# Moving loads, evictions and attention in a fused chunk-attention and swish kernel: v by whole batches, beta by rows, a 512-wide first layer at the start, attention between second layers

## The chip, the cores and the metric

The kernel runs on one core of a Trainium2 chip (trn2). The metric is the device time of one execution in microseconds (us). Executions of the kernel before vary more than most: in these studies its runs that were not marked slow lay between 333.3 and 340.1 us, and a run's time goes with the clock that TensorE was granted in it (mean 0.94 to 0.97). So every experiment below was timed against runs of the kernel before on the same chip, in the same rounds. A run is marked slow when it is more than 1.5% above the fastest of the same kernel. The clock is given as a share of full speed.

Engines are named as the profile names them: PE is TensorE (matmuls; PEld is its loading of weights), DVE is VectorE, ACT is ScalarE, POOL is GpSimd, SP is the engine that issues plain DMAs.

## The reference, cut to what matters

```python
# q, k, v: (batch 8, heads 8, seq 576, head_dim 64), float32
# attention inside chunks of 64 positions, 9 chunks per sequence
scores = (1/8) * q_c @ k_c.T            # per chunk and head, 64 x 64
attn   = softmax(scores)
x      = (attn @ v_c)                   # -> (4608 tokens, 512)
h      = x @ w_in                       # 512 -> 2048      "first layer"
g      = h * sigmoid(beta * h)          # beta: one number per hidden unit
out    = g @ w_out                      # 2048 -> 512      "second layer"
```

## The kernel before

Tokens are handled in 36 pairs of chunks (128 tokens each). Pairs are grouped in blocks: blocks 0 to 2 have 1, 1 and 2 pairs and share one tile of results, blocks 3 and 4 have 2 pairs each, and blocks 5 to 11 have 4 pairs (512 tokens). One row of a block's first layer (`emit_m`) is four matmuls for 128 hidden units. It is followed by a tanh on ACT (h * sigmoid(beta * h) is half of h * (1 + tanh(beta * h / 2)), so the kernel halves beta first) and one add-and-multiply on DVE, which I call the eviction. An attention step (`attn_step`) emits a pair's value product, and before it the scores and exponentials that it needs. `warm(n)` is n matmuls on zeros, whose results nobody uses. A pair's second layer (`emit_t`) is 16 matmuls of 512 columns.

```python
def load_vf(n, engines):                # v of one unit (2, 3 or 4 chunks), by head
    for a in range(2):
        for e in range(HS):
            for h in range(2):
                engines[i % len(engines)].dma_start(out=t[64*a:64*a+64, e, h], in_=v[...])

def emit_pv(i):                         # value product of pair i, then normalise on DVE
    ...
    if i >= EARLY:                      # EARLY = 8
        nc.sync.dma_start_transpose(out=xt_t[j][...], in_=x16...)   # DMA transpose
    else:
        x_t[i] = x16                    # later: 4 PE transposes and an ACT copy (emit_xt)

def sc_after(g):                        # after the scores of a group of three chunks
    if c == 0: load_qk(batch b+2)
    if c == 3: load_v(b+2)              # 4 DMAs on POOL, into one of three v buffers
    if c == 3: emit_T(batch b+1, first half)    # DVE transposes of q and k, 2.3 us a half
    if c == 6: emit_T(batch b+1, second half)
# main part, cut
nc.scalar.dma_start(out=beta_sb, in_=moe_beta.rearrange("(k p) -> p k", p=128))
...
ms(0, 8, 10); emit_xt(3); ms(2, 0, 8)   # ms(j, a, b): rows a to b of block j's first layer
ms(0, 10, 16); ms(1, 8, 16); ms(2, 8, 16)
...
# blocks 4 and later: attention steps are spread over first-layer rows and second layers
```

In these traces each engine takes its instructions in the order in which the program gives them (in the kernel before, ACT's first exponential, at 14.26 us, stands behind the halving of beta, at 14.13). POOL runs ahead of the others: a load that it issues waits only for its buffer to come free, and everything behind that load on POOL waits with it.

The softmax here doesn't subtract the row's maximum and nothing guards it: scores larger than these inputs give would overflow.

## Time and profile before

| | before |
|---|---|
| median of three runs | 335.48 us (335.41 to 336.15) |
| the profiled run | 338.64 us, 336.9 us of it in the span |
| PE busy | 300.8 us |
| DMA traffic | 33.2 MB, 36.7 MB read from HBM |

The profiled execution was 3 us longer than the median, though not enough to be marked slow.

From the profile page of the kernel before: the engines' busy time, and 40 slices of the span with the PE's busy share and the granted PE clock in tenths.

```profile
PE 300.8 (89%) x3130; PEld 153.3 (45%) x3130; DVE 168.8 (50%) x310; ACT 154.1 (46%) x286; POOL 52.1 (15%) x74
...
PE   6465899996738999999999998999999999999995
...
PEclk9579599997995999999999999999999999999999
```

PE is full from the middle on. The low digits are in the first five slices (to 42 us) and in the tenth to twelfth (76 to 101 us). Low PE digits are followed by a low clock.

Busy time by stretch, kernel before: stretch and its length, then busy us and counts of PE, PEld, DVE, ACT and POOL, then PE clock, DMA share and GB/s. (The share adds up the times of all packets over 16 DMA engines, so it can exceed 1.)

```profile
40.00:44.00 4.00, 4.00 (x25) 3.03 (x24) 2.00 (x5) 2.51 (x6) 0.67 (x1) 0.63 1.25 194
80.00:90.00 10.00, 7.31 (x177) 5.96 (x175) 8.60 (x16) 7.34 (x17) 4.02 (x5) 0.97 0.89 121
90.00:100.00 10.00, 4.57 (x108) 3.45 (x108) 8.44 (x19) 4.11 (x10) 0.79 (x2) 1.00 1.52 169
100.00:110.00 10.00, 7.75 (x99) 3.36 (x100) 2.87 (x5) 3.62 (x6) 0.27 (x1) 0.66 0.27 43
170.00:337.00 167.00, 159.85 (x1364) 73.69 (x1362) 75.44 (x120) 74.94 (x120) 3.41 (x4) 1.00 0.27 55
```

After 170 us PE limits. Between 80 and 100 us DVE is busy 17 of 20 us and PE only 12: DVE limits there. From 100 to 110 us no engine but PE is busy for as much as half of the time, and PE runs at clock 0.66.

The chain of waits of the kernel before, at that place: start, length, what.

```profile
92.46 0.69 DVE x_1685 L240
...
96.12 0.69 DVE x_1779 L240
...
96.83 5.37 DMA xt<-x_1779
...
102.25 1.89 PE hps L279 x4
```

The last attention result of block 5 leaves DVE at 96.8 us, its DMA transpose lands 5.4 us later, and only then can PE start block 5. Its first four matmuls take 1.89 us, twice the usual 0.86: during the idle time, at 101.0 us, the granted clock fell to 0.5.

The ACT timeline at the start of the kernel before (start, length, engine and line, what), and below it the first DVE transpose of k.

```profile
3.47 0.61 ACTq L354 DMA_DIRECT2D beta_sb<-in_moe_beta_dram  x1
...
14.13 0.22 ACT L370 ACTIVATE beta_sb<-beta_sb 128x16 f32<-128x16 f32 x1 [8.74 <-DMA beta_sb<-in_moe_beta_dram]
14.26 0.36 ACT L221 ACTIVATE et_235<-sc_201 128x256 f16<-128x256 f32 x1
```

```profile
6.92 0.63 DVE L190 STREAM_TRANSPOSE kT<-ku 128x256 f32<-128x256 f32 x1 [5.30 <-DMA ku<-in_k_dram]
```

The first q and k are there by 9 us, but the first exponential stands behind the halving of beta in ACT's order, and beta lands at 14.1 us.

### The profile page before, as it was taken

The numbers are of one execution on the slowest core, as the hardware profiler recorded it, in microseconds if no ns is written. First come the engines' busy times: TensorE is split into PE (matmuls) and PEld (weight loads), VectorE is DVE, ScalarE is ACT, GpSimd is POOL, SyncE is SP. The second block draws the span as 40 slices with busy tenths as digits, with TensorE's granted clock in tenths as the row PEclk, the third lists the DMA queues.
The fourth block names the chain that finished last, engine by engine and source line by source line (L and its number), as shares of the span: only waits on it lengthen the run. The fifth ranks groups of instructions, "written<-read, shape, count | busy, mean of one in ns | idle before, by whom it ended". The sixth has DMA issues, their size and how long they took to land.

```text
span 336.9 us, 7475 instructions
## 1 busy us (share of the span) xinstructions
PE 300.8 (89%) x3130; PEld 153.3 (45%) x3130; DVE 168.8 (50%) x310; ACT 154.1 (46%) x286; POOL 52.1 (15%) x74
## 2 busy tenths in 40 slices
PE   6465899996738999999999998999999999999995
PEld 2244585464523444444444443444444544444442
DVE  1255384567962419813871685178418604711700
ACT  1044493384543237615841672277237524823711
POOL 8352143720500500230002100000000000000000
PEclk9579599997995999999999999999999999999999
DMA  7999999999991991198012903210231113002011
GB/s 72 173 185 197 196 163 177 200 219 173 94 176 33 118 223 46 20 175 191 16 33 96 117 18 64 80 47 6 59 104 25 28 69 92 4 31 95 0 62 62
DMA packets 78450, 33.16 MB, mean 98 GB/s; under 512 B 64081, under 2 KB 70737, under 8 KB 78417
## 3 DMA queue, kind: packets, MB, share of 16 engines
q0 software_dynamic: 46080, 17.21, 46.7%
q1 hardware_dynamic: 29696, 15.34, 19.8%
q10 hardware_dynamic: 2640, 0.14, 0.6%
q8 instruction: 24, 0.39, 0.5%
q14 instruction: 10, 0.07, 0.1%
HBM read 36.71 MB, written 9.44 MB: 137 GB/s over the span
## 4 chain that ended last, share of the span: by engine, by line
PE 71%; DVE 13%; DMA 8%; ACT 2%; issue 2%; SPq 1%; ACTq 1%; DVEq 0%
PE ops L302 36%; PE hps L279 30%; DVE kT L190 4%; DVE qT L190 4%; DMA vf<-in_v_dram 3%; DMA beta_sb<-in_moe_beta_dram 3%; DVE gt L288 3%; PE x L231 2%; DMA xt<-x_1779 2%; ACT sg L287 2%; SPq L135 1%; ACTq L135 1%; PE xp L259 1%; PE wp L268 0%; DVE rd L238 0%
## 5 line engine op out<-in xcount | busy, mean ns | idle before, releaser
L279 PE MATMUL hps<-xt,w_in_104 128*128 128x512 f16 (+2 forms) x768 | 139.9, 339 | 12.5 <-DVE gt L288 5.8
L288 DVE SCALAR_TENSOR_TENSOR gt<-sg,hps 128x512 f16<-128x512 f32 (+2 forms) x192 | 103.2, 552 | 77.4 <-ACT sg L287 76.2
L287 ACT ACTIVATE sg<-hps,beta_sb 128x512 f32<-128x512 f32 (+2 forms) x192 | 108.0, 581 | 44.4 <-PE hps L279 38.7
L302 PE MATMUL ops<-w_out_105,gt 128*128 128x512 f16 x576 | 127.6, 379 | 0.0
L279 PEld LDWEIGHTS <-w_in_104 128*128 128x128 f16 x768 | 72.4, 102 | 70.4 <-issue 12.3
L302 PEld LDWEIGHTS <-gt 128*128 128x128 f16 x576 | 55.1, 98 | 64.6
L312 ACT ACTIVATE osb<-ops 128x512 f32<-128x512 f32 x36 | 21.5, 597 | 104.7 <-PE ops L302 92.8
L238 DVE RECIPROCAL rd<-x 128x8 f32<-128x8 f32 x36 | 7.0, 193 | 63.7 <-PE x L231 63.7
L190 DVE STREAM_TRANSPOSE kT<-ku 128x576 f32<-128x576 f32 (+3 forms) x18 | 20.0, 1118 | 5.3 <-DMA ku<-in_k_dram 5.3
L212 PEld LDWEIGHTS <-kT 32*64 32x64 f16 x1152 | 12.2, 109 | 19.4 <-issue 12.8
L190 DVE STREAM_TRANSPOSE qT<-qu 128x576 f32<-128x576 f32 (+3 forms) x18 | 19.7, 1104 | 1.4 <-DMA qu<-in_q_dram 1.4
L158 POOL DMA_DIRECT2D vr_107<-in_v_dram x8 | 6.8, 868 | 51.0 <-PE x L231 51.0
L268 PE MATMUL wp<-zero 128*128 128x512 f16 x26 | 11.0, 575 | 1.2 <-DVE zero L356 1.2
L158 POOL DMA_DIRECT2D vr_106<-in_v_dram x8 | 6.9, 870 | 29.9 <-PE x L231 26.7
L158 POOL DMA_DIRECT2D vr_108<-in_v_dram x8 | 6.8, 875 | 19.0 <-PE x L231 18.9
L120 POOL DMA_DIRECT2D qu<-in_q_dram x10 | 6.7, 675 | 13.7 <-DMA w_in_104<-in_moe_w_in_dram 5.9
L263 ACT COPY xt<-xp 128x512 f16<-128x512 f16 x8 | 4.7, 585 | 8.9 <-PE xp L259 8.9
L120 POOL DMA_DIRECT2D ku<-in_k_dram x10 | 7.0, 703 | 7.3 <-DMA w_out_105<-in_moe_w_out_dram 5.8
L268 PEld LDWEIGHTS <-zero 128*128 128x128 f16 x26 | 2.7, 125 | 5.0 <-issue 3.3
L114 POOL DMA_DIRECT2D ku<-in_k_dram x6 | 4.5, 745 | 1.6 <-DVE gt L288 1.1
L114 POOL DMA_DIRECT2D qu<-in_q_dram x6 | 4.5, 744 | 1.3 <-DVE gt L288 1.3
L370 ACT ACTIVATE beta_sb<-beta_sb 128x16 f32<-128x16 f32 x1 | 0.2, 217 | 8.7 <-DMA beta_sb<-in_moe_beta_dram 8.7
(259 smaller groups left out, 145.2 us busy)
## 6 DMA issues: line engine op xcount, KB each, us to landing
out_dram<-osb SPq DMA_DIRECT2D x36, 256.0 KB, 2.1
ku<-in_k_dram POOLq DMA_DIRECT2D x6, 576.0 KB, 10.3
qu<-in_q_dram POOLq DMA_DIRECT2D x6, 576.0 KB, 13.6
w_in_104<-in_moe_w_in_dram POOLq DMA_DIRECT2D x4, 512.0 KB, 11.6
w_out_105<-in_moe_w_out_dram POOLq DMA_DIRECT2D x4, 512.0 KB, 18.5
vr_108<-in_v_dram POOLq DMA_DIRECT2D x8, 144.0 KB, 7.1
vr_106<-in_v_dram POOLq DMA_DIRECT2D x8, 144.0 KB, 10.0
vr_107<-in_v_dram POOLq DMA_DIRECT2D x8, 144.0 KB, 5.8
```

Of the source, the lines that this page charges most:

```text
L114: nc.gpsimd.dma_start(out=t.rearrange("p e r d -> p e (r d)"), in_=src[b].rearrange("(e h) (p r) d -> (h p) e (r d)", h=HQ, p=32),)
L120: nc.gpsimd.dma_start(out=t[:, e], in_=src[b, e * HQ:(e + 1) * HQ, s:s + w, :].rearrange("h (p r) d -> h p (r d)", p=32),)
L158: nc.gpsimd.dma_start(out=vring[b % NVR][64 * a:64 * a + 64, e, :, :, 0:D].rearrange("p h c d -> p (h c) d"), in_=v[b, h0:h0 + 2].rearrang ...
L190: nc.vector.transpose(out=dst[n][:, sl].bitcast(FP32).rearrange("p h i r o -> p h r (i o)"), in_=a[:, sl].bitcast(FP32),)
L212: nc.tensor.matmul(out=sc[hq % 2][o0:o0 + 64, c, e, :], lhsT=kt[32 * hq:32 * hq + 32, e, cs, par], rhs=qt[32 * hq:32 * hq + 32, e, cs, par ...
L238: nc.vector.reciprocal(out=rd, in_=x[:, :, :, D:D + 1])
L268: nc.tensor.matmul(out=ps, lhsT=zero[:, 0:128], rhs=zero, start=True, stop=True)
L279: nc.tensor.matmul(out=hps, lhsT=w_in16[:, 2 * (kk % 2) + kk // 2, m * 128:(m + 1) * 128], rhs=xt_t[j][:, kk, :], start=(kk == 0), stop=(k ...
L287: nc.scalar.activation(out=sg, in_=hps, func=ACTF.Tanh, scale=beta2_sb[:, m:m + 1])
L288: nc.vector.scalar_tensor_tensor(out=gt_t[gi][:, m, col:col + n], in0=sg, scalar=1.0, in1=hps, op0=ALU.add, op1=ALU.mult,)
L302: nc.tensor.matmul(out=ops, lhsT=gt_t[gi][:, kk, col + o * 128:col + (o + 1) * 128], rhs=w_out16[:, kk, :], start=(kk == 0), stop=(kk == K ...
L312: nc.scalar.activation(out=osb, in_=ops, func=ACTF.Copy, scale=0.5)
```

## The change

Its intent is to fill the DMA engines from the first microsecond, to take beta's wait away, to save ACT and DVE instructions at the start, and to put attention where ACT and DVE are idle, which is beside second layers. The diff, cut to its core:

```diff
-    EARLY = 8
+    EARLY = 12                                   # pairs 8 to 11 too by PE transposes
-    beta_sb = const.tile([128, KFF], FP32)
+    beta_in = const.tile([32, 128], FP32)        # 16 rows of 512 B, then four 32x32
+    beta_sb = const.tile([128, 32], FP32)        # transposes and a multiply on DVE
     def load_vf(b, engines):                     # whole batch: 4 transfers of 288 KB
         for a in range(2):
             for e in range(HS):
-                for h in range(2): ... one head of one unit ...
+                engines[e % len(engines)].dma_start(out=t[64*a:64*a+64, e]..., in_=v[b, h0:h0+2]...)
...
-        ms(1, 0, 8)
         emit_T(2)
-        cast_v(2, "dve")
+        cast_v(2, nc.vector)
+        load_vf(1, [nc.sync])
+        ms(1, 0, 8)
...
-        ms(0, 8, 10)
+        warm(2)
         emit_xt(3)
         ms(2, 0, 8)
-        ms(0, 10, 16)
-        ms(1, 8, 16)
-        ms(2, 8, 16)
+        ms("all", 8, 16)                         # blocks 0 to 2 as one 512-wide product
...
-        emit_T(5, (0,))                          # (in the middle of block 3)
...
+        emit_T(5, (0,))
+        ms(4, 0, 8)
+        emit_T(5, (1,))
+        ms(4, 8, 16)                             # before: 4 attention steps inside block 4
+        for i in range(4):
+            attn_step()                          # pairs 8 to 11
+            emit_t(4 + i, 0, 9)
+            emit_xt(8 + i)
+            emit_t(4 + i, 9, 16)
         for j in range(5, NB):                   # before: attention steps spread evenly
             for m in range(KFF):
                 if m == 4:
+                    for t in pend:
+                        if npv[0] < goal: attn_step()
+                        emit_t(t)
+                elif j == 5 and m in (1, 5, 9, 12):
+                    attn_step()                  # pairs 12 to 15
+                emit_m(j, m)
```

More of the change, by code (lines that the diff above doesn't have):

```diff
@@ L44 @@
     qk_p = ctx.enter_context(tc.tile_pool(name="qk", bufs=3))
-    vf_p = ctx.enter_context(tc.tile_pool(name="vf", bufs=2))
+    vf_p = ctx.enter_context(tc.tile_pool(name="vf", bufs=1))
     qt_p = ctx.enter_context(tc.tile_pool(name="qt", bufs=2))
@@ L126, in load_qk, with load_vf @@
             dst[n] = t
-    def load_vf(n, engines):
-        b, c, cnt = units[n]
-        t = vf_p.tile([128, HS, 2, cnt, D], FP32, tag="vf", name="vf")
-        i = 0
+    def load_vf(b, engines):
+        t = vf_p.tile([128, HS, 2, BC, D], FP32, tag="vf", name="vf")
         for a in range(2):
             for e in range(HS):
-                for h in range(2):
-                    engines[i % len(engines)].dma_start(
-                        out=t[64 * a:64 * a + 64, e, h],
-                        in_=v[b, 4 * e + 2 * a + h, c * CH:(c + cnt) * CH, :].rearrange(
-                            "(c p) d -> p c d", p=CH
-                        ),
-                    )
-                    i += 1
-        v_t[n] = t
+                h0 = 4 * e + 2 * a
+                engines[e % len(engines)].dma_start(
+                    out=t[64 * a:64 * a + 64, e].rearrange("p h c d -> p (h c) d"),
+                    in_=v[b, h0:h0 + 2].rearrange("h (c p) d -> p (h c) d", p=CH),
+                )
+        v_t[b] = t
     def cast_v(n, eng):
         b, c, cnt = units[n]
-        t = v_t.pop(n)
-        for e in range(HS):
-            op = nc.gpsimd.tensor_copy if eng == "pool" else nc.vector.tensor_copy
-            op(
-                out=vring[b % NVR][:, e, :, c:c + cnt, 0:D],
-                in_=t[:, e],
-            )
+        eng.tensor_copy(
+            out=vring[b % NVR][:, :, :, c:c + cnt, 0:D].rearrange("p e h c d -> p (e h) c d"),
+            in_=v_t[b][:, :, :, c:c + cnt].rearrange("p e h c d -> p (e h) c d"),
+        )
     def load_v(b):
@@ L243, in emit_pv @@
         j, o = pair_block[i]
-        if o == 0:
+        if i == 0:
+            xs = xt_p.tile([128, KDM, 512], FP16, tag="xt", name="xt")
+            for jj in range(3):
+                xt_t[jj] = xs[:, :, blocks[jj][3]:blocks[jj][3] + blocks[jj][1] * 128]
+            xt_t["all"] = xs
+        elif i > 3 and o == 0:
             xt_t[j] = xt_p.tile([128, KDM, blocks[j][1] * 128], FP16, tag="xt", name="xt")
@@ L272, in emit_m @@
     def emit_m(j, m):
-        n = blocks[j][1] * 128
-        gi, col = blocks[j][2:]
+        n, gi, col = (512, 0, 0) if j == "all" else (blocks[j][1] * 128, *blocks[j][2:])
         if gi not in gt_t:
@@ L350, in ms, with beta_half @@
             emit_m(j, m)
+    def beta_half():
+        for g in range(4):
+            nc.vector.transpose(
+                out=beta_sb[32 * g:32 * g + 32, :], in_=beta_in[:, 32 * g:32 * g + 32]
+            )
+        nc.vector.tensor_scalar_mul(out=beta2_sb, in0=beta_sb[:, 0:KFF], scalar1=0.5)
     with tc.manual_schedule():
         load_vf(0, [nc.sync, nc.scalar])
-        nc.scalar.dma_start(out=beta_sb, in_=moe_beta.rearrange("(k p) -> p k", p=128))
-        load_vf(1, [nc.sync])
+        nc.vector.memset(beta_in, 0.0)
         nc.vector.memset(zero, 0.0)
+        nc.sync.dma_start(out=beta_in[0:KFF, :], in_=moe_beta.rearrange("(k p) -> k p", p=128))
         for i in range(NVR):
@@ L369 @@
         load_qk(3)
-        nc.scalar.activation(out=beta2_sb, in_=beta_sb, func=ACTF.Copy, scale=0.5)
+        load_qk(4)
         emit_T(0)
-        cast_v(0, "dve")
-        load_vf(2, [nc.sync])
+        cast_v(0, nc.vector)
+        beta_half()
         warm(14)
@@ L381 @@
         emit_T(1)
-        cast_v(1, "dve")
-        load_vf(3, [nc.sync])
+        cast_v(1, nc.vector)
         sc_next()
@@ L388 @@
         emit_xt(1)
+        emit_T(2)
+        cast_v(2, nc.vector)
+        load_vf(1, [nc.sync])
         ms(1, 0, 8)
-        emit_T(2)
-        cast_v(2, "dve")
         sc_next()
-        load_qk(4)
-        load_vf(4, [nc.sync])
-        cast_v(3, "pool")
+        cast_v(3, nc.gpsimd)
+        cast_v(4, nc.gpsimd)
+        load_qk(5)
+        load_v(2)
         warm(2)
@@ L400 @@
         pv_next()
-        ms(0, 8, 10)
+        warm(2)
         emit_xt(3)
         ms(2, 0, 8)
-        ms(0, 10, 16)
-        ms(1, 8, 16)
-        ms(2, 8, 16)
+        ms("all", 8, 16)
         emit_T(3)
-        load_qk(5)
-        cast_v(4, "pool")
-        load_v(2)
         for g in range(4):
@@ L436 @@
         ms(3, 14, 16)
-        emit_T(5, (1,))
+        emit_T(5, (0,))
         load_qk(6)
         load_v(3)
-        ms(4, 0, 2)
-        attn_step()
-        ms(4, 2, 6)
-        attn_step()
-        ms(4, 6, 9)
-        attn_step()
-        ms(4, 9, 11)
-        attn_step()
-        ms(4, 11, 16)
-        pend = list(range(4, 8))
+        ms(4, 0, 8)
[6 more added lines that the diff above has]
+            emit_t(4 + i, 9, 16)
+        pend = []
         for j in range(5, NB):
             goal = blocks[j + 1][0] + blocks[j + 1][1] if j + 1 < NB else NP
-            slots = []
             for m in range(KFF):
                 if m == 4:
-                    slots += [("t", t) for t in pend]
-                slots.append(("m", m))
-            need = goal - npv[0]
-            first = 1
-            span = max(1, len(slots) - 6 - first)
-            marks = {}
-            for a in range(need):
-                w = first + (a * span) // max(1, need)
-                marks[w] = marks.get(w, 0) + 1
-            for i, sl in enumerate(slots):
-                for _ in range(marks.get(i, 0)):
+                    for t in pend:
+                        if npv[0] < goal:
+                            attn_step()
+                        emit_t(t)
+                elif j == 5 and m in (1, 5, 9, 12):
                     attn_step()
-                if sl[0] == "t":
-                    emit_t(sl[1])
-                else:
-                    emit_m(j, sl[1])
+                emit_m(j, m)
             pend = list(range(blocks[j][0], blocks[j][0] + blocks[j][1]))
```

## The prediction

> **What bounds the kernel now.** From 110 us to the end TensorE is the limit: busy-by-stretch view, 160 of 167 us busy after 170 us, clock 1.00. A 512-wide matmul takes 0.216 us, so a block of four token pairs costs 13.8 us per layer; blocks take 30.5 to 32 us with attention. Most of the loss is before: TensorE is idle about 17 us of the first 50, with clock 0.5 to 0.85, and about 11 us between 70 and 105. There VectorE is the limit (8.6 of 10 us busy at 80-90). The chain of waits ends this stage in a DMA transpose (96.8 to 102.25) that leaves TensorE idle about 4.5 us and at clock 0.5 until 107.
>
> **What changes, by stage.**
>
> 1. Start. In the ACT timeline the first exponential waits for the half-beta, which waits 10.6 us for a 2048-element beta load (3.5 to 14.1). Sixteen rows of 512 B remove this. The Trainium skill (DMA: Bandwidth & Descriptors, Specifications) says transfers under 512 B fall short of line rate; 10.6 us for 8 KB agrees. But all of v (1.18 MB) now shares the DMA engines with the first q and k, so I expect the first value product at about 12.5 us, not 14.7. Then the DMA is full (about 190 GB/s to 60 us), and q of the third unit gates: it landed near 28, I expect 25-26. The transposes moved ahead of eight evictions spare part of TensorE's 2.7 us wait at 31.8. Net about 2.5 us by the third value product.
> 2. 512-wide first layer: 24 ACT and VectorE pairs (0.29 and 0.47 us on ACT, 97% busy from 44 to 52) become 8 of 0.69, and TensorE limits: 8 us become 6.9. Gain 1.3 us.
> 3. Blocks 3 and 4. Four attention steps and two whole-batch transposes (2.3 us per half) leave the first layers, where VectorE limits, for the second layers, where ACT and VectorE idle. Pairs 8 to 11 use TensorE transposes (0.4 us) instead of the late DMA transpose. From the start of block 3 (68.35) to the end of block 5's first layer I count about 69 us before and 56 after. Gain about 13.
> 4. New loss: in block 5 the attention of pair 15 stands before row 12 of 16, behind a 2.3 us VectorE transpose, and its DMA transpose (2.4 us quiet, 5 to 6 beside loads) must land in the 3.5 us of rows 12-15. TensorE should idle 3 to 6 us, with the clock falling to 0.5: loss about 6.
> 5. Steady blocks: attention before each second layer removes the VectorE/ACT stalls; blocks near 30.3 us. Gain about 4.
>
> Sum: about 15 us, nearly all on the critical path, as TensorE runs in order with little slack afterwards. Prediction 320.8 us, range 315 to 327. Faster by over 2%: 0.94; within 2%: 0.05; slower: 0.01.
>
> **What would show it.** Right: no ACT wait for beta; first value product before 13.5 us; block 3's first layer starting near 64.5; no wait for a DMA transpose before block 5; one of several us before block 6, with a clock drop; no TensorE wait on a VectorE x product in later blocks. Wrong: first score product after 12 us (v crowding q and k), third-unit transposes waiting past 29, or TensorE waiting for evictions in blocks 3 and 4 as long as before.
>
> **What would make it wrong.** v up front delaying q, k and w_in so that the start gains nothing (plus 3 us); no stall at block 6 (minus 6); evictions blocked behind the early transposes while q is in flight; v of the second batch (one buffer, copied on GpSimd) holding up the loads queued behind it.

## The result, and the profile after

| | before | after |
|---|---|---|
| median of three runs | 335.48 us (335.41 to 336.15) | 325.84 us (324.85 to 326.75) |
| ratio, 95% interval | | 0.9706 (0.9657 to 0.9755) |
| the profiled run | 338.64 us | 325.84 us |
| PE busy, mean clock | 300.8 us, 0.949 | 295.6 us, 0.963 |

A ratio is the mean time of one kernel's fast runs over that of the other's of the same rounds, so it is not quite the ratio of the medians. The kernel is 9.6 us faster. The prediction's range holds the time, but its gain of 14.7 us was half as large again as the real one.

The page of the changed kernel, as above:

```profile
PE 295.6 (91%) x3084; PEld 147.9 (46%) x3084; DVE 170.7 (53%) x297; ACT 153.8 (47%) x273; POOL 51.8 (16%) x72
...
PE   7268799987799975999999999999999999999995
...
PEclk9676999999999995999999999999999999999999
```

The deep hole of the twelfth slice is gone. There is a new one in the fifteenth and sixteenth slices, again followed by a low clock. The busy time by stretch shows both, with the columns as before:

```profile
40.00:44.00 4.00, 4.00 (x23) 1.96 (x21) 2.94 (x7) 3.08 (x7) 1.20 (x2) 1.00 1.38 183
76.00:84.00 8.00, 4.45 (x41) 3.80 (x40) 7.78 (x16) 4.28 (x11) 0.00 (x0) 1.00 1.87 180
84.00:104.00 20.00, 20.00 (x351) 10.65 (x348) 9.87 (x17) 9.17 (x19) 4.81 (x6) 1.00 1.00 145
120.00:124.00 4.00, 0.15 (x1) 0.00 (x0) 3.33 (x7) 0.69 (x2) 0.00 (x0) 0.82 1.27 157
124.00:130.00 6.00, 5.17 (x14) 1.95 (x15) 1.37 (x2) 1.51 (x3) 0.00 (x0) 0.55 0.02 4
```

In 76 to 84 us DVE is still the limit: DVE transposes of q and k (2.3 us for each half of a batch) stand among the evictions of block 4. From 84 to 104 us attention runs beside second layers and PE is never idle. From 120.2 us on PE stands still for 4.7 us; the clock falls to 0.5 at 122.6 us and stays there until 129.4 us. The chain of waits of the changed kernel says why:

```profile
118.00 1.17 DVE kT L183
119.17 1.08 DVE qT L183
...
120.31 0.69 DVE x_2120 L233
...
121.02 3.67 DMA xt<-x_2120
...
124.83 5.85 PE hps L276 x16
```

This is the stall that the prediction named. Pair 15's attention result waits for two DVE transposes, and block 6 waits for its DMA transpose. The result is there at 121.0 us, 0.85 us after block 5's last matmul, and the DMA transpose then takes 3.7 us.

At the start, the ACT and the DVE timeline of the changed kernel:

```profile
14.78 0.38 ACT L214 ACTIVATE et_224<-sc_190 128x256 f16<-128x256 f32 x1 [11.21 <-PE sc_191 L205]
```

```profile
12.65 0.63 DVE L183 STREAM_TRANSPOSE kT<-ku 128x256 f32<-128x256 f32 x1 [10.91 <-DMA ku<-in_k_dram]
```

Beta holds nothing any more, but k now lands at 12.6 us in place of 6.9, and the first exponential is half a microsecond later than before.

I cut both traces at the first matmul of each stage. The last column gives other profiles whose code in that stage is that of the kernel before, because the profile of the kernel before was a long one.

| stage, us | before | after | other profiles with the code of before |
|---|---|---|---|
| start to block 2 | 38.7 | 36.8 | 37.8, 37.4 (e1, e3) |
| block 2 to first second layer | 13.3 | 10.4 | 11.3, 11.3, 11.3 (e1, e4, e8) |
| to block 3 | 16.3 | 16.3 | |
| block 3 to the end of block 5's first layer | 68.1 | 56.6 | 68.0, 67.3 (e3, e8) |
| idle before block 6 | none | 4.7 | |
| block 6 to the end | 200.6 | 199.2 | 200.6, 200.6 (e3, e8) |

### The profile page after: what moved, and what is told of

Same layout as the page of the kernel before. It is cut to its first block, busy times and chain, and to the rows that moved or that the text cites. A ratio compares the mean times of both kernels' runs of the same rounds, so it can differ in the third digit from the quotient of the medians.

```text
span 324.1 us, 7273 instructions
## 1 busy us (share of the span) xinstructions
PE 295.6 (91%) x3084; PEld 147.9 (46%) x3084; DVE 170.7 (53%) x297; ACT 153.8 (47%) x273; POOL 51.8 (16%) x72
## 4 chain that ended last, share of the span: by engine, by line
PE 80%; DVE 9%; DMA 4%; ACT 3%; issue 1%; POOL 1%; ACTq 0%; DVEq 0%; POOLq 0%
PE ops L299 37%; PE hps L276 36%; DMA qu<-in_q_dram 3%; DVE gt L285 3%; PE x L224 2%; DVE kT L183 2%; DVE qT L183 2%; ACT sg L284 1%; DMA xt<-x_2120 1%; PE xp L257 1%; PE wp L266 1%; ACT xt L261 1%; POOL ku L121 0%; DVE rd L231 0%; DVE x_3155 L233 0%
## 5 line engine op out<-in xcount | busy, mean ns | idle before, releaser
L276 PE MATMUL hps<-xt,w_in_105 128*128 128x512 f16 (+2 forms) x704 | 133.3, 351 | 10.3 <-DMA xt<-x_2120 4.7
L299 PE MATMUL ops<-w_out_106,gt 128*128 128x512 f16 x576 | 130.3, 380 | 0.0
L284 ACT ACTIVATE sg<-hps,beta_sb 128x512 f32<-128x512 f32 (+2 forms) x176 | 105.3, 611 | 36.5 <-PE hps L276 29.0
L276 PEld LDWEIGHTS <-w_in_105 128*128 128x128 f16 x704 | 68.6, 102 | 70.7 <-issue 14.5
L299 PEld LDWEIGHTS <-gt 128*128 128x128 f16 x576 | 54.0, 98 | 61.5
L183 DVE STREAM_TRANSPOSE qT<-qu 128x576 f32<-128x576 f32 (+3 forms) x18 | 19.7, 1106 | 0.1
L205 PEld LDWEIGHTS <-kT 32*64 32x64 f16 x1152 | 11.6, 108 | 18.1 <-issue 9.5
L261 ACT COPY xt<-xp 128x512 f16<-128x512 f16 x12 | 7.0, 586 | 17.0 <-PE xp L257 17.0
L266 PE MATMUL wp<-zero 128*128 128x512 f16 x28 | 11.3, 552 | 1.3 <-DVE zero L359 1.3
L121 POOL DMA_DIRECT2D qu<-in_q_dram x10 | 6.7, 669 | 11.5 <-DVE gt L285 2.9
L121 POOL DMA_DIRECT2D ku<-in_k_dram x10 | 7.2, 726 | 5.3 <-DMA w_out_106<-in_moe_w_out_dram 2.3
## 6 DMA issues: line engine op xcount, KB each, us to landing
vr_107<-in_v_dram POOLq DMA_DIRECT2D x8, 144.0 KB, 10.2
```

The lines of the kernel that those rows point to most:

```text
L121: nc.gpsimd.dma_start(out=t[:, e], in_=src[b, e * HQ:(e + 1) * HQ, s:s + w, :].rearrange("h (p r) d -> h p (r d)", p=32),)
L183: nc.vector.transpose(out=dst[n][:, sl].bitcast(FP32).rearrange("p h i r o -> p h r (i o)"), in_=a[:, sl].bitcast(FP32),)
L205: nc.tensor.matmul(out=sc[hq % 2][o0:o0 + 64, c, e, :], lhsT=kt[32 * hq:32 * hq + 32, e, cs, par], rhs=qt[32 * hq:32 * hq + 32, e, cs, par ...
L261: nc.scalar.copy(out=xt_t[j][:, :, o * 128:(o + 1) * 128], in_=xp)
L266: nc.tensor.matmul(out=ps, lhsT=zero[:, 0:128], rhs=zero, start=True, stop=True)
L276: nc.tensor.matmul(out=hps, lhsT=w_in16[:, 2 * (kk % 2) + kk // 2, m * 128:(m + 1) * 128], rhs=xt_t[j][:, kk, :], start=(kk == 0), stop=(k ...
```

## The experiments

The prediction was a sum of five terms. The first four runs do one part of the change alone, or undo one. The next four test the reasons for what those showed. The last four put together what helped. All gave correct results. Times are medians of all runs; ratios are of fast runs alone, against the kernel before in the same rounds (one run of e3 and one of e8 were marked slow). e1 to e4 ran on one chip, e5 to e8 on a second, e9 to e11 on a third and e12 on a fourth, and the change itself was timed apart from all of them. So a difference of medians between these groups is only as good as the ratios, or the stages of the profiles, that go with it.

| run | time, us | ratio (95% interval) |
|---|---|---|
| e1 attention moves only | 327.12 | 0.9708 (0.9650 to 0.9765) |
| e2 after, rows 1, 4, 6, 8 | 323.15 | 0.9584 (0.9533 to 0.9635) |
| e3 512-wide only | 335.89 | 0.9948 (0.9888 to 1.0008) |
| e4 start only | 340.43 | 1.0087 (1.0021 to 1.0152) |
| e5 = e2 and loads held | 319.89 | 0.9540 (0.9499 to 0.9581) |
| e6 = e2 and transposes moved | 327.80 | 0.9785 (0.9727 to 0.9843) |
| e7 after, rest of v held | 333.89 | 0.9956 (0.9908 to 1.0005) |
| e8 beta by rows only | 334.27 | 0.9961 (0.9897 to 1.0025) |
| e9 = e5 and e6 | 318.73 | 0.9487 (0.9453 to 0.9521) |
| e10 = e9, v paced | 320.38 | 0.9521 (0.9486 to 0.9556) |
| e11 = e10, third batch's transposes moved | 318.90 | 0.9483 (0.9445 to 0.9521) |
| e12 = e9 with e11's last edit | 316.39 | 0.9449 (0.9401 to 0.9496) |

### e1: the attention moves alone

```diff
 (kernel before)
-    EARLY = 8
+    EARLY = 12
-    ... tail from block 3 on, as before ...
+    ... tail from block 3 on, as in the change ...
```

> The kernel before with one part alone: attention moved between second layers, whole-batch transposes moved, TensorE transposes for pairs 8 to 11. Theory (most of the gain is this part, and it also brings the new stall before block 6): about 7 to 9 us faster than before (11.5 us less between the start of block 3 and the end of block 5's first layer, 1.4 us less afterwards, 4.9 us of idle TensorE added). Rival (the gain comes from the start, and the attention move only shifts waits): within 3 us of before.

The ratio is 0.9708, the same as that of the whole change. Block 3 to the end of block 5's first layer takes 56.6 us, and PE waits 4.6 us for a DMA transpose before block 6 (total us, times, longest):

```profile
PE hps L279 <- DMA xt<-x: 4.6, 1, 4.6
```

So this part carries the gain and the new stall, and all the rest of the change adds nothing that these timings can see. (The old start is still in this kernel: its first exponential came at 11.6 us, not 14.3 as in the profile of before. The beta load's landing varies from run to run.)

### e2: pair 15 earlier

```diff
-                elif j == 5 and m in (1, 5, 9, 12):
+                elif j == 5 and m in (1, 4, 6, 8):     # (and the m == 4 branch only if pend)
```

> The changed kernel with the four attention steps of block 5 at rows 1, 4, 6 and 8 in place of 1, 5, 9 and 12. Theory (pair 15's DMA transpose is issued too late): the 4.7 us TensorE wait before block 6 goes to under 1 us, the clock stays 1.00 there, and the kernel is 5 to 7 us faster than the changed one. Rival (the transpose is held by the batch loads, whatever its place): the wait stays over 3 us.

By the medians it is faster than the change by 2.7 us, half of what I expected (by the ratios 1.3%, about 4 us; from block 2 to the end the two profiles differ by 2.6 us). The two waits on PE, of the changed kernel and of e2, from the view of who waited for whom (total us, times, longest):

```profile
PE hps L276 <- DMA xt<-x_2120: 4.7, 1, 4.7
```

```profile
PE hps L276 <- DMA xt<-x: 2.4, 1, 2.4
```

The clock stayed at 1.00 this time, and block 6 took 30.2 us in place of 32.5. But 2.4 us of waiting are left, though pair 15's attention now stands eight rows before the end of the block, and block 5's own first layer grew from 17.5 to 19.4 us. Pair 15's result was now there at 118.7 us, 4.3 us before block 5's last matmul, which would have hidden a transpose of 2.4 us. Neither theory covers this alone. The issue and landing records of the trace show the four DMA transposes of block 5's attention taking 2.5, 7.6, 10.3 and 6.5 us. Something slows them, and the same transposes took 2.4 us where nothing else moved.

### e3: the 512-wide first layer alone

```diff
 (kernel before)
-        ms(0, 8, 10); ... ms(0, 10, 16); ms(1, 8, 16); ms(2, 8, 16)
+        warm(2); ... ms("all", 8, 16)
```

> The kernel before with one part alone: rows 8 to 15 of the first layer of blocks 0 to 2 as one 512-wide product. Theory of the prediction (24 pairs of evictions become 8): 1 to 1.5 us faster than before, seen between the first 256-wide product and the first second-layer product. Rival (the 2.9 us seen there came mostly from the clock, which happened to be 1.00 instead of 0.5 after 36 us): the stretch still takes over 12 us at clock 0.5, and the time is within 1 us of before.

The stretch took 10.4 us against 11.3 us in e1, e4 and e8, which have the narrow products: 0.9 us gained. The 13.3 us of the kernel before were this profile's bad luck. Its clock was 0.63 between 40 and 44 us (the stretch above), 1.00 in the changed kernel. So both theories hold in part. The saving is real but smaller than 1.3 us, and the other 2 us between the two profiles are clock. The ratio's interval includes 1.

### e4: the start alone

```diff
 (kernel after)
-    EARLY = 12, ms("all", 8, 16), new tail
+    EARLY = 8, narrow products and the tail as before
```

> The kernel before with one part alone: v of a whole batch in four transfers up front, beta by rows, earlier transposes and load issues at the start; evictions and attention order as before. Theory: the first k transpose again starts near 12.6 us instead of 6.9, the first exponential no earlier than 14.3, block 2 starts 1 to 2 us earlier; 1 to 2 us faster than before in all. Rival (the beta wait was worth its 2 us and more): 3 us faster or more.

This kernel is slower than the one before, by 0.9%, which neither theory had. Block 2 starts at 37.0 us, 1 us earlier than the mean of 38.0 in the three profiles with the old start. The loss lies elsewhere: block 3 to the end of block 5 took 73.8 us in place of 68. With EARLY = 8, pairs 8 to 11 go by DMA transposes again, and PE waited for the last of them:

```profile
PE hps L276 <- DMA xt<-x: 11.1, 1, 11.1
```

The four transposes took 7.6, 11.8, 15.3 and 12.0 us, with batch loads in flight. In the whole change, the PE transposes of pairs 8 to 11 keep this cost away. Why the loads lay worse on these transposes than in e3 (11.6, 10.1 and 6.9 us for the last three) was not tested. The traces show one difference: when the first of the four was issued (82.1 us in e4, 81.6 in e3), a batch of q and k was still under way in e4. Its queue moved 359 packets of 2304 B from 82 to 86 us, against 73 in e3. That this is the reason is not shown.

### e5: the batch loads held back

```diff
 (e2)
+        if i == 15:          # in emit_pv, after pair 15's result
+            nc.gpsimd.tensor_copy(out=hold_sb, in_=x16[:, 0, 0, 0:1])
+            load_v(5)        # no longer issued when the scores of pair 14 are emitted
```

> The kernel with rows 1, 4, 6 and 8, and GpSimd made to read one column of pair 15's attention result before it issues the next batch of v, so that these 1.18 MB are not in flight beside the DMA transposes of pairs 13 to 15. Theory (the transposes are slow because of the batch loads in flight): the remaining 2.4 us wait before block 6 goes to under 0.5 us and the DMA transposes of pairs 14 and 15 land in 2.4 to 3 us in place of 6 and more; 2 us faster than with the rows alone. Rival (pair 15's attention result itself is late, VectorE being the limit): the wait stays over 1.5 us.

POOL issues the v of batch 5 as soon as its buffer is free, which is after pair 13's value product: in the middle of block 5's attention. The small copy makes POOL wait until pair 15's result exists, with all that stands behind it: v is issued at 117.3 us in place of 108.5, and the q and k loads that follow at 120.6 in place of 111.9. The transposes then took 2.5, 4.7, 2.4 and 2.4 us, and the wait is gone. (The one of 4.7 us had no packet of POOL's queue beside it; what slowed it stays open.) Two stretches of e5, with columns as before:

```profile
120.00:124.00 4.00, 4.00 (x20) 1.81 (x19) 3.30 (x5) 3.15 (x5) 2.10 (x3) 1.00 2.04 145
124.00:130.00 6.00, 6.00 (x103) 2.87 (x102) 3.19 (x8) 2.37 (x5) 0.76 (x1) 1.00 1.30 191
```

PE is busy throughout, at clock 1.00. The kernel is 3.3 us faster than e2 by the medians, on another chip. From block 2 to the end the profiles differ by 2.6 us, which is the wait of 2.4 us; the rest lies in the start, whose code is the same. The rival falls: pair 15's result came as late in the block as in e2 (15.2 us after block 5's start in both) and did not hold block 6. The loads in flight did. Which of them, v or the q and k behind it, was not separated.

### e6: the transposes out of block 5

```diff
 (e2)
-        if b >= 1 and c == 3: emit_T(...)      # and c == 6
+        if b >= 1 and c == 3 and b != 3: ...   # and c == 6
 ...
+        # block 6, after row 3: emit_T(first half), value product of pair 16,
+        # emit_T(second half), then second layers; the next scores one step later
```

> The kernel with rows 1, 4, 6 and 8, and the two VectorE transposes of 2.3 us each that stood in block 5 moved behind the first layer rows of block 6, beside second layers. Theory (VectorE is over its limit in block 5: 16 evictions of 0.69, 4 attention results of 0.9 and 4.7 us of transposes are 19.4 us against TensorE's 16.4): block 5's first layer takes 16.5 to 17.2 us in place of 19.4, pair 15's result comes about 2 us earlier, and the wait before block 6 falls below 1 us; 3 to 4 us faster than with the rows alone. Rival (loads in flight hold the DMA transposes whatever VectorE does): block 5 is shorter but the wait grows by as much, and the time stays within 1 us.

DVE did what I expected. Block 5's first layer took 16.9 us in place of 19.4, and pair 15's result came 3.8 us earlier, counted from block 5's start. But the DMA transposes got worse still (2.5, 7.0, 16.5 and 14.4 us):

```profile
PE hps L276 <- DMA xt<-x: 9.1, 1, 9.1
```

The kernel is slower than e2 by 4.65 us by the medians, and the intervals of the ratios lie apart; the profiled run was the slowest of six (330.61 us), so its stages may overstate the loss. The rival was right in kind, and the loss was more than it said. With DVE quicker, the transposes of pairs 14 and 15 were issued 3.9 and 6.5 us after v's first load, in place of 6.1 and 10.3 in e2, so more of the loads still lay ahead of them: a faster engine, and a slower kernel. Not all of it is explained by that: they landed 21 us after v's first load, in e2 17.

### e7: the rest of v held

```diff
 (after)
-        load_vf(0, [nc.sync, nc.scalar])
+        load_vf(0, [nc.sync, nc.scalar], 0, 2)          # chunks 0 and 1, by head
 ...
         emit_T(0)
+        nc.vector.memset(v_t[0][:, :, :, 2:BC, 0:1], 0.0)   # the DMAs wait for this write
+        load_vf(0, [nc.sync], 2, BC)
```

> The changed kernel, with v of the first unit alone (two chunks of nine) up front and the rest of v held until the first q and k have landed. Theory (v up front crowds the first q and k): the first k transpose starts near 7 us in place of 12.6, the first exponential near 10.5, the first attention result near 12 in place of 16.4, and the third comes 0.5 to 1.5 us earlier; 0.5 to 1.5 us faster than the changed kernel. Rival (the same bytes have to come by then, so all is paid back): the third attention result is within 0.3 us of 33.3 to 34.2.

The first half of the theory holds: k was transposed at 7.1 us, the first exponential came at 10.1 and the first attention result at 11.7. Then everything was lost, and 8 us more than the change. From the DVE timeline of e7:

```profile
16.96 0.82 DVE L186 STREAM_TRANSPOSE qT<-qu 128x384 f32<-128x384 f32 x1
32.05 0.56 DVE L145 CAST vr<-vf 128x768 f16<-128x768 f32 x1 [14.26 <-DMA vf<-in_v_dram]
```

The held 0.92 MB (seven ninths of 1.18 MB) were issued from 9.5 us and landed at 32 us. The packet records of the trace show how. These are counts worked out from them, for two queues: the one of POOL (q, k and the weights) and the one of SP (v).

```
us         POOL's queue: packets, median size, GB/s    SP's queue: packets, median size, GB/s
24 to 26   367  1024 B  150                            367  256 B  45
26 to 28   316  1024 B  158                            310  256 B  38
28 to 30   335  1024 B  163                            276  256 B  34
```

In this stretch the queues get nearly the same number of packets, whatever the size of a packet. The Trainium skill (DMA: Bandwidth & Descriptors, Queues, rings and completion order) says that each engine goes round its queues packet by packet, and these counts agree. (A packet of the page holds several descriptors, typically 9 to 17; whether a record of the trace is such a packet or a single descriptor, no run here shows.) So v, in packets of 256 B, gets a fifth of the bytes as long as weight packets of 1024 B are waiting. The change's transfers up front are through before the weights come. That is what they buy, and the late q and k are the price.

For a DMA transpose beside the loads, the turn by packets is only part of the account. A transpose of one pair has about 540 packets, nearly all of 256 B, on SP's queue. From 117 to 121 us of e6 the two queues moved 312 packets each, POOL's nearly all of 2304 B (q and k). But from 113 to 116 us, with two transposes or more issued and not landed, POOL's queue moved 2307 packets, most of 128 B (v), and SP's only 100. And in the changed kernel, the transpose issued at 116.2 us had its first packet 3.8 us later, beside q and k, where in e5 the last two began after 1.2 us. Turns of one packet each don't explain these stretches. That the loads slow the transposes is shown by e5; by what mechanism they hold back the first packets stays open.

### e8: beta by rows alone

```diff
 (kernel before)
-        nc.scalar.dma_start(out=beta_sb, in_=moe_beta.rearrange("(k p) -> p k", p=128))
+        nc.scalar.dma_start(out=beta_in[0:KFF, :], in_=moe_beta.rearrange("(k p) -> k p", p=128))
 ...
-        nc.scalar.activation(out=beta2_sb, in_=beta_sb, func=ACTF.Copy, scale=0.5)
+        beta_half()                       # four 32x32 transposes and a multiply on DVE
```

> The kernel before with one part alone: beta as 16 rows of 512 B and block transposes on VectorE, in the same place of the ACT queue. Theory of the prediction (4-byte elements made the load slow): it lands 3 to 5 us after its issue in place of 8 to 10.6, the first exponential starts near 10.3, limited by the first q. Rival (the load is slow because it shares the DMA engines with v, q and k and its size hardly counts): it lands 8 us or more after its issue, and the first exponential starts after 11.5 as before.

The DMA view, one line each for e8 (rows, behind four small v transfers), e1 (elements, in the same place of the queue) and the changed kernel (rows, behind large v transfers); the last number is us from issue to landing:

```profile
beta_in<-in_moe_beta_dram ACTq DMA_DIRECT2D x1, 8.0 KB, 5.1
```

```profile
beta_sb<-in_moe_beta_dram ACTq DMA_DIRECT2D x1, 8.0 KB, 8.0
```

```profile
beta_in<-in_moe_beta_dram SPq DMA_DIRECT2D x1, 8.0 KB, 10.4
```

With elements it took 8.0, 9.3 and 10.6 us in three profiles, with rows 5.1 us, so the theory of the prediction holds in size. But rows took 10.4 us as well where two v transfers of 288 KB stood ahead of them on SP's queue, so what is in flight ahead of the load or beside it counts as much (the two were not separated). In e8 the first exponential came at 10.2 us, the first attention result at 11.5, and block 2 started at 36.6 us, as early as in the changed kernel (36.8). So in this one profile the rows alone give what the change's start gives. v up front and the moved transposes add nothing to it that these profiles can see: in the six profiles with the change's start (the change, e2, e5, e6, e9 and e12) block 2 started between 35.7 and 37.7 us, 36.4 in the mean. By time the rows alone are not clear of noise: the ratio's interval includes 1.

### e9 to e12: what helped, together

> The changed kernel with rows 1, 4, 6 and 8, the held batch loads, and the two VectorE transposes moved out of block 5: both of the last two edits together. Theory (moving the transposes failed alone only because the DMA transposes then lay beside the loads; without the loads VectorE's share of block 5 counts): block 5's first layer takes about 17 us in place of 19.4, no wait before block 6, about 2 us faster than with the loads held alone, near 318. Rival (the transposes cost as much in block 6): the same as with the loads held alone.

> The kernel of the run before this one, with v of the first batch in 24 transfers by head and by unit (2, 3 and 4 chunks), paced by their issue at about 0.65 us each, in place of four large ones. Theory (four large transfers at once crowd q and k; paced ones don't, and early enough ones are done before the large weight packets take their turns): first k transpose near 7 us, first attention result near 12, third 1 us earlier than with the large transfers, 0.5 to 1.5 us faster. Rival (the later units of v get one small packet for each large weight packet, as when they were held): VectorE waits for v in the second or third copy, no gain or a loss.

> The kernel of the run before this one, with the second half of the third batch's VectorE transposes moved from the middle of block 4's first layer to beside the second layer of pair 4. Theory (VectorE limits blocks 3 and 4): their first layers take about 2 us less (19.4 in place of 21.6) and nothing is lost after, so about 2 us faster. Rival (the score products that need these transposes wait for them): the gain is lost again between the end of block 4 and block 5.

> All that helped, together: the changed kernel with v in four large transfers kept, rows 1, 4, 6 and 8, the held batch loads, the transposes out of block 5, and the third batch's second transposes beside the second layer of pair 4. Theory (the parts lie in different stages, so their gains add): blocks 3 and 4 take 19.7 us as in the run before, the rest as in the kernel with large transfers, so 1 to 2 us faster than either, 316 to 318. Rival (the start's jitter is larger than the difference): within 0.5 us of both.

```diff
 e9   e5's hold and e6's move together
 e10  e9, and v of the first batch by head and unit, all issued at once (no hold on v)
 e11  e10, and beside pair 4's second layer: value product of pair 8, emit_T(5, (1,));
      the scores that need it after pair 4's second layer
-        ms(4, 0, 8); emit_T(5, (1,)); ms(4, 8, 16)
+        ms(4, 0, 16)
 e12  e9 with the last edit of e11
```

In e9 the transposes of block 5's pairs took 2.5, 4.3, 2.7 and 2.4 us, PE did not wait before block 6, and block 5's first layer took 16.9 us. It is 1.2 us faster than e5 by the medians (another chip; from block 2 to the end the profiles differ by 1.7 us). Of the 2.5 us saved in block 5, 0.9 come back in block 6, where the moved transposes now stand (31.1 us in place of 30.2), so the edit that cost 4.65 us beside the loads helps without them.

In e10 the first attention result came at 11.7 us in place of 16.1, and the third at 34.3 in place of 33.2. DVE waited 1.4 and 2.1 us for the later units of v, and PE 1.9 us for w_in. The rival was right: all was paid back, and 1.7 us more. With e7 this makes two ways of giving q and k the first place, and both lose.

In e11 the first layers of blocks 3 and 4 took 19.7 us in place of 21.6, and the kernel was 1.5 us faster than e10. In e12 the two add up: 316.39 us, 18.8 us less than the kernel before in the same rounds and, by ratios, 2.6% less than the change. Blocks 3 and 4 took 19.7 us in it, and block 5's first layer 16.9.

## Why the prediction was right or wrong, point by point

The mechanism of the largest term was right, and e1 confirms it alone; so were those of the 512-wide layer and of the steady blocks. At the start the crowding by v was under-sized, and of the stall only one of two causes was given its weight. The time lies in the range, 1.2 us below its end. The sum was 5 us too large because every gain was over-sized, by 0.3 to 1.5 us, and the stall under-sized by 1.

| term | predicted | measured | from |
|---|---|---|---|
| start | -2.5 | -1.2 | 36.8 against the mean of 38.7, 37.8 and 37.4 (-1.5 with the mean of the six profiles named at e8; single profiles spread by 2) |
| 512-wide first layer | -1.3 | -0.9 | 10.4 against 11.3 in e1, e4 and e8 |
| block 3 to the end of block 5's first layer | -13 | -11.5 | 56.6 against 68.1 |
| stall before block 6 | +6 | +7 | 4.7 idle, and 2.3 more for block 6 at the low clock (32.5 against 30.2 in e2) |
| steady blocks | -4 | -3.7 | 199.2 less these 2.3, against 200.6 |
| sum | -14.8 | -10.3 | the timed runs say -9.6 |

- **Start.** "I expect the first value product at about 12.5 us": it came at 15.6. The crowding was named, but its size was taken too small. The first score product came after 12 us, which the prediction had listed as the sign that it is wrong. The gain that was left is what beta's rows give alone (e8, one profile); nothing shows a share of v in it.
- **Beta.** "10.6 us for 8 KB agrees" was too quick. The Trainium skill's statement (DMA: Bandwidth & Descriptors, Specifications) that transfers under 512 B fall short of line rate fits e8, but the 10.6 us held a share of queueing as well: rows took 10.4 us behind v.
- **512-wide.** The mechanism holds. The difference of 2.9 us between the two profiles is no measure of it, as 2 us of that are clock.
- **Blocks 3 and 4.** Confirmed by e1 in place and size. DVE was the limit there and still is in the changed kernel (7.78 of 8 us busy), which e11 and e12 used.
- **The new stall.** It came where and as foretold, with the clock at 0.5. The reason given, "must land in the 3.5 us of rows 12-15", fits the changed kernel: pair 15's result came after the last of these rows, and its transpose took 3.7 us. Against the quiet 2.4 us the loads make, by estimate, 1.3 of the 4.7 us there. But the place was only half of the cure. Moving the steps earlier (e2) left 2.4 us, and easing DVE after that made it worse (e6). Holding the loads as well removed it (e5). The prediction had the loads as a detail ("5 to 6 beside loads"); once the steps stood earlier they were the cause of what was left. The hold was not tried with the steps at their old rows.
- **Steady blocks.** Confirmed: blocks 7 and 8 took 30.6 and 30.8 us in place of 32.1 and 32.6. Blocks 9 and 10 took 30.1 in both kernels.

The profile of the kernel before had run 3 us over its median. Stage times read from it carried this into the difference of the two profiles (12.8 us, against 9.6 us timed).

## What to carry to other kernels

Ask of each DMA that something waits for which queue with larger packets it will meet: in e7 the queues took turns by packet, and v in packets of 256 B got a fifth of the bytes beside packets of 1024 B; a DMA transpose took up to 16.5 us beside bulk loads in place of 2.4. A load that starts as soon as its buffer is free starts at a moment that nobody chose, and one small instruction that makes its issuer wait can be worth more than a faster engine. Measure the parts of a bundle alone: here one part carried the whole gain, one hurt alone, and one that hurt alone helped once another was there.

## What the Trainium skill lacked or had wrong

- DMA: Bandwidth & Descriptors, Queues, rings and completion order: the turn by packets is stated, and the runs agree (367 and 367 packets in 2 us). What follows from it for mixed traffic is not: in e7 0.92 MB in packets of 256 B took 22 us beside a queue with 1024 B packets. Nor do turns explain every stretch: from 113 to 116 us of e6 the queue of the pending DMA transposes moved 100 packets, the other 2307.
- DMA: Bandwidth & Descriptors, DMA Transpose (X-bar), and VectorE: DVE Perf Modes, The three transpose paths: the second gives 1309 ns for a 128x128 tile, and neither says how much a DMA transpose depends on other traffic. A 128x512 f16 tile took 2.4 us alone and up to 16.5 us beside batch loads (e6). By the transposes on PE it took 0.4 us there and 0.59 us for the copy on ACT.
- TensorE: Matmul & The Clock Gate, What's actually happening: half clock after at least one idle window of about 3.4 us. The runs show the fall, but 3.4 us is no safe limit: in the changed kernel the clock fell to 0.5 when PE had been idle for 2.4 us (120.15 to 122.57 us, by the trace's modelled ends of matmuls), in the kernel before at 77.1 us after an idle time of 1.7 us, and in e1 only 5.2 us after the last matmul. An idle time of 2.4 us in e2 left it at 1.00.
- DMA: Bandwidth & Descriptors, Specifications: transfers below 512 B are slow. The runs agree for beta (8.0 to 10.6 us by elements, 5.1 us by rows), but position in the queue changed the same load as much (10.4 us for rows behind v), which the section doesn't speak of.
